# Dividing the probabilities by their sum before they are split and turned, in a top-k attention followed by two feed-forward layers

## The chip, the cores and the metric

The kernel runs on one core of a Trainium2 chip. The metric is the device time of one execution, in microseconds. It is written for a planner that puts every engine's instructions in an order of its own, from priorities and a model of costs, and sets the waits between engines; each engine then works through its own queue strictly in that order. The engines are TensorE (PE, with PEld for the loading of weights), VectorE (DVE), ScalarE (ACT), GpSimd (POOL) and SyncE (SP), which issues the DMAs.

## The reference

Three steps follow each other. Attention over 4 batches x 8 heads x 576 positions x 64, in which each row keeps its 32 largest scores; then two feed-forward layers on the 2304 rows of 512.

```
scores = (q @ k.T) / 8
kth    = 32nd largest of each row
attn   = exp(where(scores >= kth, scores, -1e9) - max)
attn   = attn / (sum(attn) + 1e-9)
x      = heads of (attn @ v) side by side          # 2304 x 512
x      = (sigmoid(x @ w_gate) * (x @ w_val)) @ w_out   # inner size 1536
out    = relu(x @ w_in)**2 @ w_out2                    # inner size 2048
```

## The kernel before

The 2304 rows are 18 row blocks of 128. Six chunks of one block come first, then six chunks of two blocks (`CHUNKS`). A chunk goes through attention and then through the two layers. Attention works in units: one row block and one head, eight per block, 144 in all. Heads go in pairs (j = 0 and 1), because two heads of 64 fill 128 partitions.

A unit has these steps. `head` loads what is needed and calls `scores` (L349): f32 matmuls, and ScalarE copies the 128x576 scores into a score tile `S` (L371). `softmax` (L374) lets VectorE look for the 32 largest: four times MAX8 (L383), three times MATCH_REPLACE8 (L390). `marks` keeps these four MAX8. Then GpSimd makes the threshold (L398) and the offset (L399), ScalarE masks (L402, Prelu) and takes the exponential.

From chunk 6 on (`TCI`), that is in the last 96 units, the probabilities are not divided there. GpSimd adds 10 ln 2 to the offset (L406), ScalarE takes the exponential twice, once as f16 into the unit's own score tile (L412) and once as f32 with its sum (L413). GpSimd subtracts one from the other, in two pieces (L417, L420), so that the score tile holds a high and a low f16 part. A DMA that turns the tile writes it into `PT` (L436). After the second head of a pair GpSimd scales both sums by a factor of the values (L427).

`tail` for two units earlier calls `values16` (L494): VectorE takes one over the two sums (L499), TensorE multiplies the turned probabilities with the values (L508), and then spreads the two inverse sums over 64 partitions each with f32 matmuls against the identity (L520). ScalarE copies product and spread (L529), GpSimd multiplies them (L531), and the result is split in two f16 parts (L533, L534).

In the early chunks (0 to 5) the probabilities are divided at once: exponential with sum, GpSimd, reciprocal on VectorE (L444), product on GpSimd (L453).

The layers (`moe`, L787) work on 256 inner columns at a time: `l1_pair` makes the gate and value products (L766) and a tile of activations in two f16 parts (L781, L782), `l1_acc` multiplies it into the chunk's second input (L806). `l2_pair` and `l2_acc` do the same for layer two (L869, L878 to L882, L890). The tiles of activations have the tag `hi`, with `HIB` of them; output tiles `ob` (L907) use the same tag. Between the layers the input is measured and split (L837 to L848), and `nxt`, from chunk `PRE0` on, starts the first two column pairs of the next chunk in that place.

The order of the work is set by emission and priority. The units of attention are emitted ahead of the layers: `LEAD` units ahead of the chunk that is in the layers, `LEAD2` from chunk `PRE0` on. Within a unit, `late` emits the next unit's `head`, pending splits of values, and the `tail` of two units ago, all of it with higher priority than the unit's own threshold and exponential. Two marks hold things back in the order: the reciprocal not before the second MAX8 of the unit that is searched (`marks[1]`), the value matmuls not before its last (`marks[3]`).

Score tiles have the tag `S`, with `SB` of them; the staging of keys and values (`prep_keys` L145, `prep_values` L186) uses the same tag.

Of the kernel before, what the change touches and what calls it, by code (L numbers as in the profile page):

```python
# [2 lines left out]

# [6 lines left out]
F16 = mybir.dt.float16  # L10
BF16 = mybir.dt.bfloat16
F32 = mybir.dt.float32
# [3 lines left out]
AF = mybir.ActivationFunctionType  # L16
ALU = mybir.AluOpType
# [5 lines left out]
P = 128  # L23
# [1 line left out]
NEG = -3.0e38  # L25
BIG = float(2.0**100)
M4 = 3
HIB = 3
DEPTH2 = 2
CHUNKS = [[0], [1], [2], [3], [4], [5]] + [[i, i + 1] for i in range(6, 18, 2)]  # L30
AHEAD = 1000
LEAD = 9
CA0 = -5.0
CA = 6.0
CW = 3.0
# [3 lines left out]
PLAIN = (0,)  # L39
KST = 3  # L40
NPRE = 2
PRE0 = 6
X2W = 3
LEAD2 = 14
TD = 7
# [17 lines left out]
LOP = 3  # L63
LOA = 0
TCI = 6
SB = 4
XRB = 1
PB = 10

# [5 lines left out]
def tile_topk_attention__then__two_moe_layers(  # L75
# [14 lines left out]
    nc = tc.nc  # L90
    B, H, S, D = q.shape
# [6 lines left out]
    NHP = H // 2  # L98
# [19 lines left out]

    ident = const.tile([P, P], F32, name="ident")
    make_identity(nc, ident)  # L120
    ones = const.tile([P, P], BF16, name="ones")
    nc.vector.memset(ones, 1.0)


    def pow2_scale(norm, name, pool=mpool, tag=None, bufs=None, squared=True, s=None):
# [130 lines left out]
    def xfac(ci, b):  # L256


        if ci not in xfacs:
            bs_ = batches(ci)  # L260
            vf = vsc.bitcast(F32)
            ix = mpool.tile([P, 1], F32, tag="xsc", bufs=3, name=f"ix_{ci}")
            nc.vector.reduce_max(ix, vf[:, bs_[0] * NHP : (bs_[-1] + 1) * NHP, 1], axis=AX.X)

            nc.gpsimd.tensor_scalar(ix, ix, 2.0, None, op0=ALU.mult)
            fs = {}
            for b_ in bs_:
                f = mpool.tile([P, NHP], F32, tag="xfc", bufs=4, name=f"xfc_{ci}_{b_}")
                nc.gpsimd.tensor_scalar(
                    f, vf[:, b_ * NHP : (b_ + 1) * NHP, 0], ix, 1.0, op0=ALU.mult, op1=ALU.mult  # L270
                )
                fs[b_] = f
            xfacs[ci] = ix, fs
        return xfacs[ci][1][b]

    class Pair:


        def __init__(self, ci, hp, xt):
            self.ci, self.hp, self.xt = ci, hp, xt  # L280
            self.tts = chunks[ci]
            self.N = len(self.tts) * P
            self.segs = segments(ci)
            self.vt, self.kt, self.qt, self.pt, self.ends, self.sums = {}, {}, {}, {}, {}, {}

        def load(self):
            ci, hp = self.ci, self.hp
# [86 lines left out]
        def softmax(self, j, i, ss, late=None):  # L374
# [26 lines left out]
            )  # L401
            nc.scalar.activation(wk, ss, AF.Prelu, bias=bs[:, 0:1], scale=1.0, alpha=BIG)  # L402
            if self.ci >= TCI:


                nc.gpsimd.tensor_scalar(  # L406
                    bs[:, 1:2], bs[:, 1:2], float(PB * math.log(2.0)), None, op0=ALU.add
                )
                if j == 0:
                    self.sums[i] = apool.tile([P, 2], F32, tag="rz", bufs=3, name=f"z_{tt}_{self.hp}")  # L410
                pp = ss.bitcast(F16)
                nc.scalar.activation(pp[:, 0:S], wk, AF.Exp, bias=bs[:, 1:2], scale=SCALE)  # L412
                nc.scalar.activation(  # L413
                    wk, wk, AF.Exp, bias=bs[:, 1:2], scale=SCALE,
                    accum_out=self.sums[i][:, j : j + 1],
                )
                nc.gpsimd.tensor_tensor(  # L417
                    pp[:, S + ST : 2 * S], wk[:, 0:SM], pp[:, 0:SM], op=ALU.subtract
                )
                nc.gpsimd.tensor_tensor(  # L420
                    pp[:, S : S + ST], wk[:, SM:S], pp[:, SM:S], op=ALU.subtract
                )
                if j == 1:

                    z = self.sums[i]
                    for b, _, o, n in pieces(tt):
                        nc.gpsimd.tensor_scalar(  # L427
                            z[o : o + n],
                            z[o : o + n],
                            float(1e-9 * 2.0**PB),  # L430
                            xfac(self.ci, b)[o : o + n, self.hp : self.hp + 1],
                            op0=ALU.add,
                            op1=ALU.mult,
                        )
                pt = apool.tile([P, 2 * CB + 1, P], F16, tag="PT", bufs=3, name=f"PT_{tt}_{h}")
                nc.sync.dma_start_transpose(pt, pp)  # L436
                self.pt[(j, i)] = pt
                return None
# [13 lines left out]
            for o, x in ((self.ends[i][:, j], wk[:, SM:S]), (wk[:, 0:SM], wk[:, 0:SM])):  # L452
                nc.gpsimd.tensor_scalar(o, x, rz, 1.0, op0=ALU.mult, op1=ALU.mult)  # L453
            return wk, ident

        def transpose(self, j, i, wk, dg):
            tt = self.tts[i]
# [33 lines left out]
                )  # L491
                nc.scalar.copy(self.pe[:, i * P : (i + 1) * P], tq[:, 0:P])

        def values16(self, i, after=None, summed=None):  # L494
            tt = self.tts[i]
            xp = ps_t.tile([P, 512], F32, tag="tr", name=f"xp_{tt}_{self.hp}")

            z = self.sums[i]
            rc = nc.vector.reciprocal(z, z)  # L499
            if summed is not None:  # L500
                tc.add_manual_dep(rc.ins, summed.name, NOSYNC, reason="summed by then")

            terms = [(a, c, c) for c in range(CB + 1) for a in range(2)]
            terms += [(0, c, CB + 1 + c) for c in range(CB)]
            for b, _, o, n in pieces(tt):
                for x, (a, c, pc) in enumerate(terms):
                    for j in range(2):
                        mm = nc.tensor.matmul(  # L508
                            xp[j * D : (j + 1) * D, o : o + n],
                            self.vt[b][:, j, a, c],  # L510
                            self.pt[(j, i)][:, pc, o : o + n],
                            start=(o == 0 and x == 0),
                            stop=(x == len(terms) - 1),
                            skip_group_check=True,
                        )
                        if after is not None:
                            tc.add_manual_dep(mm.ins, after.name, NOSYNC, reason="lands by then")
                            after = None
            for j in range(2):
                nc.tensor.matmul(  # L520
                    xp[j * D : (j + 1) * D, P : 2 * P],
                    z[:, j : j + 1].to_broadcast([P, D]),
                    ident,
                    start=False,
                    stop=True,
                    skip_group_check=True,
                )
# [182 lines left out]
    def split_act(src, name, xs, N):  # L710

        sq = xs[:, 1].bitcast(BF16)
        nc.scalar.activation(sq, src, AF.Square)
        pq = ps_t.tile([P, 512], F32, tag="tr", name=name + "pq")
        for c in range(KM):
            nc.tensor.matmul(pq[:, 0:N], ones, sq[:, c], start=(c == 0), stop=(c == KM - 1))
        cm = mpool.tile([P, 1], F32, tag="xcm", bufs=2, name=name + "cm")
# [69 lines left out]
    def moe(ci, nxt=None):  # L787
# [45 lines left out]
        with tc.high_priority(offset=XUP):  # L833
            sq = x2[:, 1].bitcast(BF16)
            pq = ps_w.tile([P, 512], F32, tag="wk", name=f"x2pq_{ci}")
            for h in range(2):
                nc.scalar.activation(sq[:, h * KH : (h + 1) * KH], srcs[h], AF.Square)  # L837
                for c in range(h * KH, (h + 1) * KH):
                    nc.tensor.matmul(pq[:, 0:N], ones, sq[:, c], start=(c == 0), stop=(c == KM - 1))
            cm = mpool.tile([P, 1], F32, tag="cm", bufs=2, name=f"x2cm_{ci}")  # L840
# [181 lines left out]
    def attention():  # L1022
# [55 lines left out]
                nxt = pairs[pi + 1]  # L1078
                nxt.queries(nxt.tts[0:1])

        def tail(n, after=None, summed=None):
            pr, pi, j, i = units[n]
            if pr.ci >= TCI and j == 0:
                return
# [21 lines left out]
                        )  # L1106
            pr.xt = xts[pr.ci]
            if pr.ci >= TCI:
                pr.values16(i, after, summed)
# [14 lines left out]
        for n, (pr, pi, j, i) in enumerate(units):  # L1124
# [18 lines left out]
            work[n] = pr.softmax(j, i, ready.pop(n), late)  # L1143
            yield
        for n in range(len(units) - 2, len(units)):
            tail(n)
        yield
# [51 lines left out]
    for ci in PLAIN:  # L1199
        n = 0  # L1200
# [92 lines left out]
```

## Time and profile before

| | |
|---|---|
| median of 3 runs | 1302.67 us (1301.55 to 1307.42) |
| profiled execution, its own time | 1302.77 us |
| its span | 1301.0 us |
| PE busy | 1185.3 us (91%) |
| DVE busy | 978.3 us (75%) |
| POOL busy | 852.3 us (66%) |
| ACT busy | 816.7 us (63%) |
| granted TensorE clock, mean | 0.95 |

The span is the time from the first to the last instruction that the profiler saw. Busy time of an engine is the union of its instructions. A wait in the lists is idle time of an engine ahead of an instruction, put down to the event that came last. Lines as L520 are lines of the kernel before. A f32 matmul is recorded as two. Shares of busy time are means over stages; the stages differ here, as the rows show.

### The profile page before, as it was taken

To read this page: it belongs to the slowest core of one execution; us is meant where nothing else is said; L and a number is where in the kernel's file an instruction comes from. 1 tells how busy PE (TensorE), PEld (TensorE's weight loads), DVE (VectorE), ACT (ScalarE), POOL (GpSimd) and SP (SyncE) were. 2 spreads that over 40 slices of the span, in tenths; PEclk is the share of its full clock that TensorE was granted. 3 is DMA by queue.
4 is the path that set the end of the run, shared out by engine and by line. 5 is a ranking of instruction groups with operands and counts; after the bars stand their busy time and mean duration, and the time that the engine had idled before them with its cause. 6 is when DMAs were issued, how large, how long until landed. Compare 5 with 4: busy or idle time off the path is not lost.

```text
span 1301.0 us, 31666 instructions
## 1 busy us (share of the span) xinstructions
PE 1185.3 (91%) x11901; PEld 955.4 (73%) x11901; DVE 978.3 (75%) x1954; ACT 816.7 (63%) x1714; POOL 852.3 (66%) x1450
## 2 busy tenths in 40 slices
PE   6756989878999898998988999999999999999998
PEld 5545877666888778786877778867876887787775
DVE  6999989999759978799879779999999976010010
ACT  4877777777667676767666766767677656222122
POOL 1888879877657486767666867787678657315223
PEclk9557999988999999998999999999999999999999
DMA  7979762222454355555566556446544523100000
GB/s 185 348 264 307 248 180 63 73 64 76 135 143 114 96 138 138 128 136 115 146 132 135 118 142 136 115 113 175 95 98 102 117 44 51 26 2 1 17 1 17
DMA packets 243194, 154.00 MB, mean 118 GB/s; under 512 B 193120, under 2 KB 209504, under 8 KB 243040
## 3 DMA queue, kind: packets, MB, share of 16 engines
q1 hardware_dynamic: 243040, 151.97, 44.7%
q8 instruction: 94, 1.54, 0.5%
q14 instruction: 60, 0.49, 0.1%
HBM read 105.51 MB, written 18.09 MB: 95 GB/s over the span
## 4 chain that ended last, share of the span: by engine, by line
PE 55%; DVE 12%; POOL 11%; DMA 8%; ACT 6%; issue 5%; SPq 2%; POOLq 0%; ACTq 0%; DVEq 0%
PE ph L869 11%; PE acc L890 10%; PE pv L766 7%; PE pg L766 7%; PE acc L806 7%; PE sp L368 5%; DVE mx L383 4%; DVE W L390 3%; DMA PT<-S 3%; POOL S L417 2%; PE xp L508 2%; PE xp L546 2%; DMA wg_r<-in_moe_w_gate_dram 2%; POOL rh L882 1%; ACT W L413 1%
## 5 line engine op out<-in xcount | busy, mean ns | idle before, releaser
L383 DVE MAX8 mx<-W 128x8 f32<-128x576 f32 x432 | 327.5, 758 | 10.6
L869 PE MATMUL ph<-x,wi_w 128*128 128x256 f16 (+1 forms) x2112 | 210.6, 254 | 9.5 <-ACT x L845 8.3
L390 DVE MATCH_REPLACE8 W<-mx,W 128x576 f32<-128x576 f32 x288 | 213.8, 742 | 0.0
L869 PEld LDWEIGHTS <-wi_w 128*128 128x128 f16 x2112 | 172.9, 100 | 40.7 <-issue 11.6
L890 PE MATMUL acc<-w_w,rh 128*128 128x512 f16 x816 | 195.5, 379 | 1.9 <-POOL rh L882 1.9
L402 ACT ACTIVATE W<-S,bs 128x576 f32<-128x576 f32 x144 | 111.6, 775 | 105.2 <-POOL bs L398 104.6
L417 POOL TENSOR_TENSOR S<-W,S 128x512 f16<-128x512 f32 x96 | 111.3, 1159 | 80.2 <-ACT W L413 79.2
L766 PE MATMUL pg<-xs,wg_w 128*128 128x256 f16 (+1 forms) x1584 | 156.4, 249 | 1.1 <-POOL xs L534 1.1
L766 PE MATMUL pv<-xs,wv_w 128*128 128x256 f16 (+1 forms) x1584 | 154.7, 249 | 0.6 <-ACT th L776 0.4
L368 PE MATMUL sp<-kst,qt 128*128 128x288 f32 x608 | 136.8, 339 | 16.1 <-ACT S L371 4.6
L778 DVE TENSOR_TENSOR th<-pv,th 128x512 f32<-128x512 f32 (+1 forms) x66 | 37.1, 562 | 137.6 <-PE pv L766 126.5
L766 PEld LDWEIGHTS <-wg_w 128*128 128x128 f16 x1584 | 126.5, 98 | 18.5 <-issue 2.4
L806 PEld LDWEIGHTS <-wo_w 128*128 128x128 f16 x1584 | 127.5, 99 | 14.2 <-issue 2.0
L766 PEld LDWEIGHTS <-wv_w 128*128 128x128 f16 x1584 | 125.3, 98 | 15.3 <-issue 2.4
L890 PEld LDWEIGHTS <-rh 128*128 128x128 f16 x816 | 77.0, 98 | 77.4 <-POOL rh L882 2.2
L371 ACT COPY S<-sp 128x576 f32<-128x576 f32 x144 | 91.4, 635 | 61.2 <-PE sp L368 33.5
L806 PE MATMUL acc<-gh,wo_w 128*128 128x128 f16 (+1 forms) x1344 | 126.1, 247 | 0.8 <-POOL gh L782 0.6
L383 DVE MAX8 mx<-S 128x8 f32<-128x576 f32 x144 | 107.2, 744 | 24.2 <-ACT S L371 22.7
L368 PEld LDWEIGHTS sp<-kst,qt 128*128 128x128 f32 x608 | 94.8, 201 | 28.8 <-ACT S L371 8.1
L881 POOL TENSOR_TENSOR r<-r 128x512 f32<-128x512 f32 (+1 forms) x88 | 74.3, 845 | 62.7 <-ACT rh L880 61.7
L390 DVE MATCH_REPLACE8 W<-mx,S 128x576 f32<-128x576 f32 x144 | 106.9, 742 | 0.0
L882 POOL TENSOR_TENSOR rh<-r,rh 128x512 f16<-128x512 f32 (+1 forms) x88 | 83.3, 948 | 4.2
(304 smaller groups left out, 2240.5 us busy)
## 6 DMA issues: line engine op xcount, KB each, us to landing
kst<-ks SPq DMA_DIRECT2D x112, 288.0 KB, 3.1
v<-vd SPq DMA_DIRECT2D x32, 320.0 KB, 3.3
qn<-in_q_dram SPq DMA_DIRECT2D x128, 64.0 KB, 2.3
wi_r<-in_moe_w_in_dram SPq DMA_DIRECT2D x16, 512.0 KB, 5.2
w_r<-in_moe_w_out_dram SPq DMA_DIRECT2D x16, 512.0 KB, 4.6
v<-in_v_dram SPq DMA_DIRECT2D x56, 128.0 KB, 2.3
wg_r<-in_moe_w_gate_dram SPq DMA_DIRECT2D x12, 512.0 KB, 8.5
wv_r<-in_moe_w_val_dram SPq DMA_DIRECT2D x12, 512.0 KB, 6.9
```

The source lines that it names most:

```text
L368: nc.tensor.matmul(sp[:, e, 0:HALF], l, r, start=(x == 0), stop=(x == len(ops) - 1))
L371: nc.scalar.copy(ss.rearrange("p (e s) -> p e s", e=2), sp[:, :, 0:HALF])
L383: m8 = nc.vector.max(mx[:, r], cur)
L390: nc.vector.match_replace(wk, mx[:, r], cur, NEG)
L402: nc.scalar.activation(wk, ss, AF.Prelu, bias=bs[:, 0:1], scale=1.0, alpha=BIG)
L417: nc.gpsimd.tensor_tensor(pp[:, S + ST : 2 * S], wk[:, 0:SM], pp[:, 0:SM], op=ALU.subtract)
L766: nc.tensor.matmul(pp[:, e * N : (e + 1) * N], wblk(wd, a, c, f0, P), xs[:, b_, c, :], start=(e == 0 and n == 0), stop=(n == 3 * KM - 1), ...
L806: nc.tensor.matmul(acc[:, d // 2, (d % 2) * N : (d % 2 + 1) * N], wblk("wo", a, f, d * P, P), gh[:, b_, e * N : (e + 1) * N], start=(f == ...
L869: nc.tensor.matmul(ph[:, e * N : (e + 1) * N], wblk("wi", a, c, f0, P), x2[:, b_, c, :], start=(e == 0 and n == 0), stop=(n == 3 * KM - 1) ...
L881: nc.gpsimd.tensor_tensor(r, r, r, op=ALU.mult)
L882: nc.gpsimd.tensor_tensor(gh[:, 1], r, gh[:, 0], op=ALU.subtract)
L890: nc.tensor.matmul(acc2[:, i, 0:DM], gh[:, b_, e * N + i * P : e * N + (i + 1) * P], wblk("w2", a, f, 0, DM), start=(f == 0 and x == 0), s ...
```

## The change

In the last 96 units the f32 exponential with its sum is taken first and alone. GpSimd scales the unit's own sum at once. A new step, `turn16`, comes one unit later: a reciprocal on VectorE, not before the third MAX8 of the next unit (`marks[2]`); a copy to f16 on ScalarE with the inverse as its scale; the same product in f32 on GpSimd, in place; the two subtractions and the turning DMA as before. The value matmuls then give the final result up to a power of two, so that the spread of the inverse sums over the partitions (L520) and its product (L531) are gone, and two ScalarE copies with a constant scale take their place.

With it come other sizes: five score tiles instead of four, two tiles of activations instead of three, a column of ones that is broadcast instead of a 128x128 tile, one buffer instead of two for two small maxima, a result tile of half the size, `LEAD` 10 instead of 9, and `PRE0` 4 instead of 6.

```
-HIB = 3
+HIB = 2
-LEAD = 9
+LEAD = 10
-PRE0 = 6
+PRE0 = 4
-SB = 4
+SB = 5
...
-    ones = const.tile([P, P], BF16, name="ones")
-    nc.vector.memset(ones, 1.0)
+    one = const.tile([P, 1], BF16, name="ones")
+    nc.vector.memset(one, 1.0)
+    ones = one.to_broadcast([P, P])
...
             if self.ci >= TCI:
-                nc.gpsimd.tensor_scalar(
-                    bs[:, 1:2], bs[:, 1:2], float(PB * math.log(2.0)), None, op0=ALU.add
-                )
...
-                nc.scalar.activation(pp[:, 0:S], wk, AF.Exp, bias=bs[:, 1:2], scale=SCALE)
...
+                nc.scalar.activation(
+                    wk, wk, AF.Exp, bias=bs[:, 1:2], scale=SCALE, accum_out=bs[:, 2:3]
+                )
+                for b, _, o, n in pieces(tt):
+                    nc.gpsimd.tensor_scalar(
+                        bs[o : o + n, 3:4], bs[o : o + n, 2:3], 1e-9,
+                        xfac(self.ci, b)[o : o + n, self.hp : self.hp + 1],
+                        op0=ALU.add, op1=ALU.mult,
+                    )
+                return ss, wk, bs
...
+        def turn16(self, j, i, ss, wk, bs, summed):
+            tt = self.tts[i]
+            h = 2 * self.hp + j
+            rz = apool.tile([P, 1], F32, tag="rz", bufs=3, name=f"rz_{tt}_{h}")
+            rc = nc.vector.reciprocal(rz, bs[:, 3:4])
+            if summed is not None:
+                tc.add_manual_dep(rc.ins, summed.name, NOSYNC, reason="summed by then")
+            pp = ss.bitcast(F16)
+            nc.scalar.activation(pp[:, 0:S], wk, AF.Copy, scale=rz)
+            nc.gpsimd.tensor_scalar(wk, wk, rz, 1.0, op0=ALU.mult, op1=ALU.mult)
+            for o, f, e in ((S + ST, 0, SM), (S, SM, S)):
+                nc.gpsimd.tensor_tensor(pp[:, o : o + e - f], wk[:, f:e], pp[:, f:e], op=ALU.subtract)
+            pt = apool.tile([P, 2 * CB + 1, P], F16, tag="PT", bufs=3, name=f"PT_{tt}_{h}")
+            nc.sync.dma_start_transpose(pt, pp)
+            self.pt[(j, i)] = pt
...
-            z = self.sums[i]
-            rc = nc.vector.reciprocal(z, z)
...
-            for j in range(2):
-                nc.tensor.matmul(
-                    xp[j * D : (j + 1) * D, P : 2 * P],
-                    z[:, j : j + 1].to_broadcast([P, D]),
-                    ident,
...
-            xr = apool.tile([P, 2 * P], F32, tag="xr", bufs=XRB, name=f"xr_{tt}_{self.hp}")
-            nc.scalar.copy(xr, xp[:, 0 : 2 * P])
-            xf = xr[:, 0:P]
-            nc.gpsimd.tensor_tensor(xf, xf, xr[:, P : 2 * P], op=ALU.mult)
+            xf = apool.tile([P, P], F32, tag="xr", bufs=XRB, name=f"xf_{tt}_{self.hp}")
             hi, lo = (self.xt[:, a, self.hp, i * P : (i + 1) * P] for a in range(2))
-            nc.scalar.copy(hi, xf)
+            for t in (hi, xf):
+                nc.scalar.activation(t, xp[:, 0:P], AF.Copy, scale=float(2.0**-PB))
             nc.gpsimd.tensor_tensor(lo, xf, hi, op=ALU.subtract)
...
                 def late(marks, n=n, pr=pr):
+                    if units[n - 1][0].ci >= TCI:
+                        turn(n - 1, marks[2])
                     if pr.ci >= TCI:
                         head(n + 1)
...
-                        tail(n - 2, marks[3], marks[1])
+                        tail(n - 2, marks[3])
```

## Rows read from the trace of the kernel before

**Rows 1.** Windows, all engines: stretch, length, busy us (count) of each, clock, DMA, GB/s.
```profile
0.00:325.00 325.00, 253.91 (x2084) 206.40 (x2085) 301.31 (x540) 237.00 (x462) 245.88 (x293) 0.84 0.57 181
325.00:488.00 163.00, 155.62 (x2049) 133.18 (x2047) 127.09 (x299) 111.56 (x282) 106.92 (x232) 0.98 0.47 125
488.00:1106.00 618.00, 589.01 (x6306) 473.54 (x6304) 537.10 (x1089) 423.76 (x900) 439.47 (x866) 0.99 0.52 118
1106.00:1301.00 195.00, 186.82 (x1472) 142.24 (x1470) 12.78 (x27) 44.39 (x73) 60.05 (x62) 0.99 0.04 11
```

**Rows 2.** Waits, 488 to 1106 us: who waited for whom, us, times, longest.
```profile
POOL S L417 <- ACT W L413: 79.2, 50, 4.5
ACT W L402 <- POOL bs L398: 75.1, 54, 3.0
...
ACT S L371 <- DMA PT<-S: 17.3, 19, 2.4
...
PE sp L368 <- ACT S L371: 4.6, 10, 0.7
...
PE kpt L164 <- DMA kn<-in_k_dram: 4.4, 3, 2.3
...
PE sp L368 <- DMA kst<-ks: 4.0, 2, 2.3
...
PE ph L869 <- ACT x L845: 3.5, 1, 3.5
```

**Rows 3.** Timeline of PE around one pair of heads: start us, us, instruction.
```profile
646.45 0.39 PE L520 MATMUL xp<-ident,z 128*64 128x128 f32 x4
646.76 0.79 PE L368 MATMUL sp<-kst,qt 128*128 128x288 f32 x4
```

**Rows 4.** Instructions on the sums `z`: count, ns min/median/max.
```profile
L520 PE MATMUL xp<-ident,z x192: 272/275/422, 484.6 to 1113.1; 128*64 128x128 f32 x192
L427 POOL TENSOR_SCALAR z<-z,xfc x52: 258/265/268, 477.5 to 1107.5; 128x2 f32<-128x2 f32 x44, 64x2 f32<-64x2 f32 x8
```

**Rows 5.** Groups by line and form, 488 to 1106 us: busy us, mean ns, idle before.
```profile
L417 POOL TENSOR_TENSOR S<-W,S 128x512 f16<-128x512 f32 x92 | 106.6, 1159 | 80.2 <-ACT W L413 79.2
...
L413 ACT ACTIVATE W<-W,bs 128x576 f32<-128x576 f32 x92 | 71.6, 778 | 1.2
...
L420 POOL TENSOR_TENSOR S<-W,S 128x64 f16<-128x64 f32 x91 | 27.8, 306 | 0.0
...
L531 POOL TENSOR_TENSOR xr<-xr 128x128 f32<-128x128 f32 x46 | 21.0, 456 | 10.8 <-ACT xr L529 9.5
...
L406 POOL TENSOR_SCALAR bs<-bs 128x1 f32<-128x1 f32 x92 | 19.9, 217 | 7.7
```

**Rows 6.** Line L453, the product of the early chunks.
```profile
L453 POOL TENSOR_SCALAR W<-W,rz x32: 684/692/697, 227.0 to 456.7; 128x512 f32<-128x512 f32 x32
```

**Rows 7.** Line L444, the reciprocal of the early chunks, and its engine's wait (us, times).
```profile
L444 DVE RECIPROCAL rz<-bs x48: 138/154/166, 22.0 to 455.4; 128x1 f32<-128x1 f32 x48
...
  POOL bs L443: 10.1, 10
```

**Rows 8.** Timeline of all engines, one unit's end and the next unit's search.
```profile
638.83 0.76 DVE L383 MAX8 mx<-W 128x8 f32<-128x576 f32 x1
...
643.06 0.78 ACT L402 ACTIVATE W<-S,bs 128x576 f32<-128x576 f32 x1 [2.56 <-POOL bs L398]
...
643.49 0.75 DVE L383 MAX8 mx<-W 128x8 f32<-128x576 f32 x1
...
646.33 0.19 ACT L413 ACTIVATION_READ_ACCUMULATOR W<-W,bs 128x1 f32 x1
```

**Rows 9.** Line L383, MAX8 on the working copy, whole span.
```profile
L383 DVE MAX8 mx<-W x432: 737/761/764, 13.6 to 1099.6; 128x8 f32<-128x576 f32 x144
```

**Rows 10.** DMA issues: count, median us from issue to landing.
```profile
PT<-S SPq DMA_TRANSPOSE x96, 2.9
```

**Rows 11.** Chain that ended last, one piece in the last stage: start, us.
```profile
1186.67 2.62 PE ph L869 x24
```

More of the change, by code (lines that the diff above doesn't have):

```diff
@@ L1 @@
-import math
 from contextlib import ExitStack
@@ L269, in xfac @@
                 nc.gpsimd.tensor_scalar(
-                    f, vf[:, b_ * NHP : (b_ + 1) * NHP, 0], ix, 1.0, op0=ALU.mult, op1=ALU.mult
+                    f,
+                    vf[:, b_ * NHP : (b_ + 1) * NHP, 0],
+                    ix,
+                    float(2.0**-PB),
+                    op0=ALU.mult,
+                    op1=ALU.mult,
                 )
@@ L283, in __init__ @@
             self.segs = segments(ci)
-            self.vt, self.kt, self.qt, self.pt, self.ends, self.sums = {}, {}, {}, {}, {}, {}
+            self.vt, self.kt, self.qt, self.pt, self.ends = {}, {}, {}, {}, {}
         def load(self):
@@ L403, in softmax @@
             if self.ci >= TCI:
-                nc.gpsimd.tensor_scalar(
-                    bs[:, 1:2], bs[:, 1:2], float(PB * math.log(2.0)), None, op0=ALU.add
-                )
-                if j == 0:
-                    self.sums[i] = apool.tile([P, 2], F32, tag="rz", bufs=3, name=f"z_{tt}_{self.hp}")
-                pp = ss.bitcast(F16)
-                nc.scalar.activation(pp[:, 0:S], wk, AF.Exp, bias=bs[:, 1:2], scale=SCALE)
-                nc.scalar.activation(
-                    wk, wk, AF.Exp, bias=bs[:, 1:2], scale=SCALE,
-                    accum_out=self.sums[i][:, j : j + 1],
-                )
[L417 to L423, printed above, removed]
-                    z = self.sums[i]
[L426 to L438, printed above, removed]
+                nc.scalar.activation(
+                    wk, wk, AF.Exp, bias=bs[:, 1:2], scale=SCALE, accum_out=bs[:, 2:3]
+                )
+                for b, _, o, n in pieces(tt):
+                    nc.gpsimd.tensor_scalar(
+                        bs[o : o + n, 3:4],
+                        bs[o : o + n, 2:3],
+                        1e-9,
+                        xfac(self.ci, b)[o : o + n, self.hp : self.hp + 1],
+                        op0=ALU.add,
+                        op1=ALU.mult,
+                    )
+                return ss, wk, bs
             nc.scalar.activation(
@@ L492, in transpose, with values16 @@
                 nc.scalar.copy(self.pe[:, i * P : (i + 1) * P], tq[:, 0:P])
-        def values16(self, i, after=None, summed=None):
+        def values16(self, i, after=None):
             tt = self.tts[i]
             xp = ps_t.tile([P, 512], F32, tag="tr", name=f"xp_{tt}_{self.hp}")
-            z = self.sums[i]
-            rc = nc.vector.reciprocal(z, z)
-            if summed is not None:
-                tc.add_manual_dep(rc.ins, summed.name, NOSYNC, reason="summed by then")
             terms = [(a, c, c) for c in range(CB + 1) for a in range(2)]
@@ L716, in split_act @@
             nc.tensor.matmul(pq[:, 0:N], ones, sq[:, c], start=(c == 0), stop=(c == KM - 1))
-        cm = mpool.tile([P, 1], F32, tag="xcm", bufs=2, name=name + "cm")
+        cm = mpool.tile([P, 1], F32, tag="xcm", bufs=1, name=name + "cm")
         nc.vector.reduce_max(cm, pq[:, 0:N], axis=AX.X)
@@ L839, in moe @@
                     nc.tensor.matmul(pq[:, 0:N], ones, sq[:, c], start=(c == 0), stop=(c == KM - 1))
-            cm = mpool.tile([P, 1], F32, tag="cm", bufs=2, name=f"x2cm_{ci}")
+            cm = mpool.tile([P, 1], F32, tag="cm", bufs=1, name=f"x2cm_{ci}")
             nc.vector.reduce_max(cm, pq[:, 0:N], axis=AX.X)
@@ L1079, in head, with turn, tail @@
                 nxt.queries(nxt.tts[0:1])
-        def tail(n, after=None, summed=None):
+        def turn(n, summed=None):
+            pr, pi, j, i = units[n]
+            pr.turn16(j, i, *work.pop(n), summed)
+        def tail(n, after=None):
             pr, pi, j, i = units[n]
@@ L1108, in tail @@
             if pr.ci >= TCI:
-                pr.values16(i, after, summed)
+                pr.values16(i, after)
             else:
@@ L1140, in late @@
                     if units[n - 2][0].ci >= TCI:
-                        tail(n - 2, marks[3], marks[1])
+                        tail(n - 2, marks[3])
             work[n] = pr.softmax(j, i, ready.pop(n), late)
             yield
+        turn(len(units) - 1)
         for n in range(len(units) - 2, len(units)):
```

4 lines of the change are left out of this document (removed).

## The prediction

> **What bounds the kernel now.** I read the stages first: busy time of each engine in four stretches [rows 1]. The reader is to see that two engines share the role. Up to 325 us VectorE is busy 301.3 of 325 us and TensorE waits for it (253.9 us busy, granted clock 0.84). From 325 us on TensorE is the bound: 155.6 of 163 us, then 589.0 of 618 us while the twelve later row blocks go through attention, then 186.8 of 195 us with nothing but the two layers. VectorE in the long third stage is at 537.1 of 618 us, so it has 80.9 us to spare there and TensorE only 29.0 us. After 325 us, then, time is TensorE's work plus its waits: taking a matmul away there pays in full as long as no new wait fills the hole, and a busier ScalarE (423.8 us) or GpSimd (439.5 us) costs only what reaches TensorE as a wait.
>
> Next the list of waits in the third stage [rows 2]. The reader is to see two kinds. The long ones are between ScalarE and GpSimd: GpSimd stands 79.2 us ahead of the split of the probabilities (L417) until the second exponential is summed, ScalarE 75.1 us ahead of L402 until GpSimd has made the threshold. They are two sides of one loop through two in-order queues, and they do not reach TensorE as such. The short ones do: score matmuls behind the copy of scores that waits for a score tile (4.6 us), the turning of keys behind its load (4.4 us), score matmuls behind the keys' load (4.0 us), and the start of layer two behind L845 (3.5 us).
>
> The third view is the timeline of TensorE at one pair of heads, and the count of the matmuls that go [rows 3, 4].
>
> **The change part by part.**
>
> *The spread of one over the sums.* Per row block and pair of heads two f32 matmuls go (L520), four records. In the queue they hold the next matmul from 646.45 to 646.76 us, 0.31 us. The trace has 192 records, 48 such groups: 48 x 0.31 = 14.9 us less for TensorE, all of it in the stage where it is the bound. I take it whole: -14.9 us.
>
> *The same division on other engines.* Per unit (row block and head, 96 of them) ScalarE keeps its count: one exponential with sum instead of two, and a scaled copy to f16 of the same 128x576 in place of the one that went; L413 shows 778 ns for that size [rows 5]. After the value matmuls there are two 128-column copies where there were one of 256 columns and one of 128: no gain that I count. GpSimd loses the add L406 (0.217 us) per unit and the product L531 (0.456 us) per pair [rows 5], and gains the product of 128x576 by one over the sum. The nearest row is the same operation on 128x512 in the early chunks, 692 ns [rows 6]; by columns 0.78 us. It also scales the sum per unit instead of per pair: 52 more instructions at 0.265 us [rows 4]. Together 96 x (0.78 - 0.217) + 52 x 0.265 - 48 x 0.456 = 54.0 + 13.8 - 21.9 = +45.9 us on GpSimd, which has 178.5 us to spare in the stage. Its cover is that spare time: nothing, if it stays off TensorE's path; the loop below is what it costs if the cover is gone.
>
> VectorE does 96 reciprocals instead of 48: 48 x 0.15 = 7 us [rows 7], inside its 80.9 us.
>
> Weighed against a rule: MAX8 and MATCH_REPLACE fill VectorE, and L383 takes 737 to 764 ns over 432 of them while GpSimd is busy seven tenths of the time [rows 9]. So no search here was held for the length of a GpSimd product. The Trainium skill, "SBUF — State Buffer", section "SBUF: two separate sides", says that GpSimd and VectorE take a shared pair of ports in turn, each for a whole instruction, and that it concerns VectorE operations with two SBUF inputs or in a two-port mode. If the searches came under it, the new products could hold VectorE for up to 96 x 0.78 = 75 us; by the row they hold it for none, and the sum goes by the row.
>
> *The added wait.* The reciprocal of a unit now stands in VectorE's queue behind the third maximum of the next unit, and behind it stand that unit's last replacement and maximum. Look at one unit [rows 8]: its last maximum ends at 639.6 us, its sum is there at 646.5 us, and the next unit's third maximum ends at 644.2 us. Without the second exponential (0.78 us) and the wait between the two, the sum would be there at about 643.06 + 0.78 + 0.97 = 644.8, scaled by 645.1 us: 0.9 us later than the earliest place of the reciprocal. So the bounds are 0 (put after the last replacement or maximum) and 96 x 0.9 = 86 us of VectorE. The nearest row is the reciprocal L444 of the early chunks, the same chain of exponential, GpSimd and reciprocal: 10.1 us of waiting in 48 [rows 7], 0.21 us each. For 96 that is 20 us. TensorE shows 29.0 us idle where VectorE shows 80.9, 0.36 of it, so I charge 0.36 x 20 = +7 us (bounds 0 and 0.36 x 86 = 31).
>
> ScalarE's scaled copy waits for the reciprocal, and behind it in ScalarE's queue stands the copy of the next scores, for which the next search waits; what that costs is part of the same +7. GpSimd's product in place, the two subtractions and the turning DMA come after. SP's queue holds its DMA issues in order too, so loads issued behind a turning DMA shift with it; the chain is longer by 0.15 + 0.78 + 0.78 - 0.78, about 0.9 us, against the value matmuls that come two units later: no cost counted.
>
> *Five score tiles.* A score tile is held until its turning DMA has landed, 2.9 us after issue [rows 10]. The added links hold it about 1 to 2 us longer; the fifth tile gives a whole unit more, 618/92 = 6.7 us. The key and value staging uses the same tiles. TensorE's waits that hang on them are the 4.6, 4.4 and 4.0 us above, 13.0 us. Bounds: 0 (these loads are late for other reasons) to 13.0; I take half, -6.5 us.
>
> *Two tiles of activations.* A pair of layer two takes 2.62 us of matmuls for the first product [rows 11] and about as much for the second, in turn. With two tiles the square of pair n must wait until the second product of pair n-2 has ended, one such stretch after its own matmuls; its result is wanted four stretches, 10.5 us, after them. Square, product and difference in that time are cheap (below 3.5 us: three operations of at most L417's 1.16 us). Cost 0, up to 0.5 us at each of 11 chunk ends (5.5 us) if the cover is gone, because the output tiles share them.
>
> *Earlier start of the next chunk (chunks 4 and 5 too), one unit more of lead.* The first two column pairs of the next chunk fill the gap before layer two. The gap it can fill is that of 3.5 us [rows 2], one single stall ahead of layer two; bounds 0 to 3.5, I take -2. Loss: the order of units against layers moves, but TensorE is the bound there and the work is the same. In the first stage more tiles and more lead may shift work; VectorE has 23.7 us idle there, I take 0 and keep a third of that, 8 us, on either side. The broadcast column of ones and the single small buffers: 0.
>
> Sum: the profiled execution took 1302.8 us (span 1301.0 plus 1.8), which is within 0.2 us of the median 1302.67. 1302.8 - 14.9 - 6.5 - 2 + 7 = 1286.4. **1286 us.** Its own range, with the terms of the tiles, the stall and the wait going either way, is 1278 to 1294.
>
> **Rivals.**
>
> *Everything frees up.* All 13.0 us and all 3.5 us go and the reciprocal costs nothing: 1302.8 - 14.9 - 13.0 - 3.5 = 1271. For it: the waits on score tiles are many (19 of ScalarE for the turning DMA, 17.3 us). Against: keys also wait for loads and stores of their own.
>
> *The hole is filled.* TensorE does 14.9 us less and waits that much more, since VectorE's pace holds it: 537.1 + 7 + 20 = 564 of then 603 us still leaves 39 us, which speaks against; that the searches stand in strict order speaks for. The score tiles' -6.5 goes against the wait's +7, and only the -2 is left: 1301.
>
> *The loop becomes the pace (slower).* One loop through the queues: reciprocal 0.15, copy 0.78, product 0.78, subtractions 1.16 and 0.31, threshold 0.22, Prelu 0.78, exponential with sum 0.97, scaled sum 0.27, and the reciprocal again: 5.4 us [rows 4 to 8], the threshold taken as L406, and with an estimated 0.07 us between neighbours (10 of them) 6.1 us. It closes only if a unit's threshold stands behind the previous unit's subtractions in GpSimd's queue. GpSimd's other work, (439.5 + 45.9)/92 - 2.74 = 2.5 us per unit, can lie in it: 6.1 to 8.6 us, against 6.7 - 0.16 = 6.56 us that TensorE then needs per unit. It decides from 6.56 us on. The loop of now, 4.2 us bare, is already closed in 50 of 92 units (the count of the 79.2 us). At the middle, 7.35 us, 50 units lose 0.8 us each, 40 us: 1302.8 - 14.9 - 6.5 + 40 = 1321. For it: the two long waits [rows 2]. Against: where the reciprocal is late the threshold can stand first, and the loop is open.
>
> **How the numbers follow.** Forecast 0.42, everything frees up 0.20, hole filled 0.16, loop 0.22. No change means within 0.5%, 6.5 us, about what a measurement of this kernel can tell: 1296 to 1309. Faster: the forecast nearly whole and the first rival, 0.62; same: the hole filled, less a little on either side, 0.15; slower: the loop and a worse front, 0.23. The range runs from just below the first rival, with some of the front's 8 us, to most of the loop's price: 1262 to 1318.
>
> **What would show it.** Right: no f32 matmul after the value matmuls; TensorE's busy time in attention of the later chunks down by about 15 us and its idle time not above 29; few waits of the score copy on the turning DMA; a GpSimd product near 0.78 us; VectorE waiting for the scaled sum some 20 us in all. The loop: VectorE waiting far more than that at the reciprocal, score copies late, TensorE idle ahead of score and value matmuls by tens of us, the last search ending after 1106 us. The forecast is wrong if TensorE's idle time rises by 15 us or more, or if the first 325 us move by more than 8.

## The result and the profile after

| | before | after |
|---|---|---|
| median of 4 runs | 1303.82 us (1301.55 to 1307.42) | 1290.03 us (1285.39 to 1293.53) |
| ratio | | 0.989, 95% interval 0.985 to 0.993 |
| profiled execution, span | 1301.0 us | 1287.5 us |

The forecast was 1286 us, faster. The profiled execution of after took 1289.27 us. Run again beside other kernels, after had the ratio 0.9866 (0.985 to 0.9883) to before.

First the stretches of after, as in [rows 1] (busy us and count of PE, PEld, DVE, ACT, POOL; clock; DMA; GB/s).

```profile
0.00:325.00 325.00, 251.85 (x2041) 204.17 (x2042) 299.55 (x540) 235.61 (x458) 241.45 (x290) 0.84 0.57 181
325.00:488.00 163.00, 155.60 (x2053) 131.37 (x2051) 127.77 (x301) 110.30 (x279) 106.53 (x229) 1.00 0.45 118
488.00:1106.00 618.00, 594.57 (x6222) 476.16 (x6220) 536.96 (x1135) 423.25 (x907) 485.65 (x878) 0.99 0.54 119
1106.00:1287.50 181.50, 173.49 (x1402) 133.64 (x1399) 12.77 (x27) 42.83 (x71) 56.10 (x59) 0.99 0.04 13
```

The reader is to see where the 13.5 us of span went. They do not show in the pace of attention: VectorE is busy 537.0 us in the third stretch as before, and the last search ends at 1101.0 us (1100.4 before). TensorE does more in the same 618 us, 594.6 us against 589.0, although it has less to do per unit: it gets further ahead with the layers, and what is left of them after attention is 181.5 us instead of 195.0. So the freed time is cashed in at the end.

Fewer matmuls are not the whole of it. After 325 us TensorE is idle 38.8 us in after and 44.5 us before (length less busy time, over three rows), 5.7 us less. And its granted clock is higher: after 325 us the clock records show the lower of the two levels for 14.3 us instead of 27.3, with TensorE busy in 12.4 and 25.2 us of them. The same layer matmul (128x256) starts every 109 ns at the upper level and every 213 ns at the lower, so an estimated 6.4 us came back there, half of the difference. A second profiled execution of after has 37.8 us idle and 11.4 us busy at the lower level.

The waits of after in the third stretch, as in [rows 2]: first of all engines, then of TensorE alone.

```profile
ACT S L450 <- DVE rz L446: 41.7, 45, 2.3
POOL W L451 <- ACT S L450: 38.6, 32, 2.9
ACT W L407 <- POOL bs L403: 35.8, 43, 2.6
...
ACT S L376 <- DMA PT<-S: 14.9, 14, 2.0
```
```profile
PE xp L505 <- DMA PT<-S: 7.7, 3, 3.8
PE sp L373 <- DMA kst<-ks: 3.5, 3, 1.6
PE kpt L164 <- DMA kn<-in_k_dram: 3.2, 4, 1.3
PE acc L876 <- POOL rh L868: 2.7, 2, 2.1
...
PE ph L855 <- ACT x L831: 0.6, 1, 0.6
PE sp L373 <- ACT S L376: 0.2, 1, 0.2
```

L505 is the line of the value matmuls, L446 the new reciprocal, L450 the scaled copy, L451 the product, L376 the copy of scores. The old loop between GpSimd and ScalarE (79.2 and 75.1 us) has become a chain over three engines with shorter waits. On TensorE the waits for score tiles and keys went from 13.0 to 6.9 us, and a new one stands at the top: value matmuls waiting for turned probabilities (5.6 us in the second profiled execution of after).

The new chain of one unit, and the wait at its end, in the timeline (all engines, 681.4 to 690 us), with the stretch behind the wait:

```profile
681.46 0.16 DVE L446 RECIPROCAL rz<-bs 128x1 f32<-128x1 f32 x1 [0.18 <-POOL bs L414]
...
681.71 0.78 ACT L450 ACTIVATE S<-W,rz 128x576 f16<-128x576 f32 x1 [1.00 <-DVE rz L446]
...
682.67 0.74 POOL L451 TENSOR_SCALAR W<-W,rz 128x576 f32<-128x576 f32 x1
...
683.59 1.42 POOL L453 TENSOR_TENSOR S<-W,S 128x512 f16<-128x512 f32 x2
...
685.04 1.31 SPq L455 DMA_TRANSPOSE PT<-S  x1
...
685.25 0.24 PE L505 MATMUL xp<-PT,v 128*64 128x128 f16 x1
...
689.26 1.02 PE L505 MATMUL xp<-PT,v 128*64 128x128 f16 x19 [3.77 <-DMA PT<-S]
```
```profile
689.50:696.30 6.80, 5.63 (x46) 4.00 (x41) 6.60 (x14) 4.60 (x11) 4.99 (x10) 0.50 0.55 131
```

From the reciprocal to the landing that releases TensorE are 7.8 us. The first value matmul has the first head's tile; the second head's is still on its way. The wait costs twice: right behind it the granted clock is at its lower level (0.50) for 6.8 us. Over the 96 units (each one's end of search against the landing of its turning DMA, both from the timeline) the median from search to landing is 14.0 us, against 10.3 us before.

### The profile page after: what moved, and what is told of

The parts are those of the page before. It is cut to its first block, busy times and chain, and to the rows that moved or that the text cites. A ratio compares the mean times of both kernels' runs of the same rounds, so it can differ in the third digit from the quotient of the medians.

```text
span 1287.5 us, 31379 instructions
## 1 busy us (share of the span) xinstructions
PE 1175.5 (91%) x11709; PEld 945.3 (73%) x11709; DVE 977.1 (76%) x2002; ACT 812.0 (63%) x1714; POOL 889.7 (69%) x1454
## 3 DMA queue, kind: packets, MB, share of 16 engines
q1 hardware_dynamic: 243040, 151.97, 45.9%
## 4 chain that ended last, share of the span: by engine, by line
PE 50%; DVE 20%; POOL 8%; DMA 8%; issue 6%; ACT 5%; SPq 2%; POOLq 0%; ACTq 0%; DVEq 0%
PE ph L855 11%; PE acc L876 10%; DVE mx L388 8%; DVE W L395 7%; PE pv L752 6%; PE pg L752 6%; PE acc L792 6%; PE sp L373 4%; PE xp L505 3%; DMA PT<-S 2%; PE xp L532 2%; DMA ve<-in_v_dram 1%; DMA vd<-vom 1%; POOL S L453 1%; POOL rh L868 1%
## 5 line engine op out<-in xcount | busy, mean ns | idle before, releaser
L855 PE MATMUL ph<-x,wi_w 128*128 128x256 f16 (+1 forms) x2112 | 206.6, 251 | 5.1 <-ACT x L831 4.5
L876 PE MATMUL acc<-w_w,rh 128*128 128x512 f16 x816 | 198.5, 380 | 5.5 <-POOL rh L868 5.5
L373 PE MATMUL sp<-kst,qt 128*128 128x288 f32 x608 | 136.2, 335 | 12.9 <-DMA kst<-ks 4.5
L453 POOL TENSOR_TENSOR S<-W,S 128x512 f16<-128x512 f32 x192 | 136.7, 734 | 2.1
L376 ACT COPY S<-sp 128x576 f32<-128x576 f32 x144 | 91.7, 637 | 55.8 <-PE sp L373 38.0
L867 POOL TENSOR_TENSOR r<-r 128x512 f32<-128x512 f32 (+1 forms) x88 | 74.3, 845 | 63.4 <-ACT rh L866 57.5
L792 PE MATMUL acc<-gh,wo_w 128*128 128x128 f16 (+1 forms) x1248 | 114.3, 244 | 1.1 <-POOL gh L768 0.8
L450 ACT ACTIVATE S<-W,rz 128x576 f16<-128x576 f32 x96 | 74.4, 775 | 48.7 <-DVE rz L446 44.9
```

Source lines behind the costliest of these rows:

```text
L373: nc.tensor.matmul(sp[:, e, 0:HALF], l, r, start=(x == 0), stop=(x == len(ops) - 1))
L376: nc.scalar.copy(ss.rearrange("p (e s) -> p e s", e=2), sp[:, :, 0:HALF])
L450: nc.scalar.activation(pp[:, 0:S], wk, AF.Copy, scale=rz)
L453: nc.gpsimd.tensor_tensor(pp[:, o : o + e - f], wk[:, f:e], pp[:, f:e], op=ALU.subtract)
L792: nc.tensor.matmul(acc[:, d // 2, (d % 2) * N : (d % 2 + 1) * N], wblk("wo", a, f, d * P, P), gh[:, b_, e * N : (e + 1) * N], start=(f == ...
L855: nc.tensor.matmul(ph[:, e * N : (e + 1) * N], wblk("wi", a, c, f0, P), x2[:, b_, c, :], start=(e == 0 and n == 0), stop=(n == 3 * KM - 1) ...
```

## The experiments

Each was timed beside before on the same chip, and ratios are to before. The runs took three chips. After itself ran again on one of them, beside experiments 7 and 9 and the second half of 4; its 0.9866 is used throughout, so elsewhere a difference to it goes across chips. With the 0.989 of the first measurement such differences are some 3 us smaller.

**1. The sizes alone.** Before, with all sizes of after.

```
-HIB = 3  LEAD = 9   PRE0 = 6  SB = 4
+HIB = 2  LEAD = 10  PRE0 = 4  SB = 5     (and the column of ones, single small buffers)
```

> The kernel before with all sizes of the kernel after (five score tiles, two tiles of activations, LEAD 10, PRE0 4, column of ones, single small buffers), the division as before. Theory A (the gain is TensorE's matmuls of the spread; sizes only trim waits): 1296 to 1303 us against 1303.8 of before. Theory B (the sizes make the gain, the moved division gives nothing): 1288 to 1293 us.

0.9943 (0.9921 to 0.9966), 1297.6 us. This is theory A's range, but the sizes are clearly worth something: 0.57% of 1304 us, 7.4 us.

**2. The division with the old sizes.** The column of ones and the single small buffers stay as in after.

```
-HIB = 2  LEAD = 10  PRE0 = 4  SB = 5
+HIB = 3  LEAD = 9   PRE0 = 6  SB = 4     (in the kernel after)
```

> The kernel after with the old sizes of four (score tiles 4, activations 3, LEAD 9, PRE0 6). Theory A: 16 us of matmuls are gone but score tiles are held some 4 us longer with one tile less: 1292 to 1299 us. Theory B: 1302 to 1308 us.

1.021 (1.0188 to 1.0232), 1332.5 us: slower than before by more than either theory allowed. The moved division needs something among the sizes.

**3. Which size it needs.** After with four score tiles, all else as it is.

```
-SB = 5
+SB = 4
```

> The kernel after with four score tiles instead of five, all else as after. If the longer hold of a score tile (the turned tile lands 14.0 us after the search in the middle of 96 units, 10.3 us before) is what made the division with the old sizes slow: ratio to before 1.008 to 1.022. If the old order or the third tile of activations did that: 0.987 to 0.995.

1.0233 (1.0216 to 1.0251), just above the range of the first theory. It is the fifth tile. The stretch of attention and the waits of four_tiles:

```profile
488.00:1106.00 618.00, 560.05 (x5780) 450.64 (x5780) 496.12 (x1052) 390.99 (x845) 442.33 (x811) 0.95 0.53 116
```
```profile
ACT S L376 <- DMA PT<-S: 57.5, 35, 4.0
```
```profile
PE sp L373 <- ACT S L376: 17.7, 9, 4.9
PE kpt L164 <- DMA kn<-in_k_dram: 14.6, 6, 4.8
PE xp L505 <- DMA PT<-S: 10.5, 6, 4.0
```

One of these waits of the score matmuls, and the stretch behind it:

```profile
597.54 0.79 PE L373 MATMUL sp<-kst,qt 128*128 128x288 f32 x4 [3.68 <-ACT S L376]
```
```profile
598.30:618.80 20.50, 10.48 (x87) 7.78 (x87) 17.34 (x35) 10.64 (x24) 12.81 (x26) 0.50 0.43 98
```

The copy of scores waits 57.5 us for tiles that the turning DMA still reads, and TensorE is busy only 560.1 us. A count fits it: from the copy into a score tile to the landing of its turning DMA are 22.2 us in the median before and 25.8 us after; with a unit every 6.7 us, that is 3.3 and 3.9 tiles held, and the staging of keys and values wants tiles of the same kind. Four were enough for the old chain and are not for the new one. The clock adds to the loss: right behind the wait shown it falls to 0.50 for 20.5 us, and it is 0.95 in the whole stretch. TensorE is idle 58.0 us of the 618 (23.4 in after) and busy 43.0 us at the lower level (9.1 in after), by the spacing of the matmuls above an estimated 17 us lost (half of the difference).

**4. The order alone, both ways.** After with the old lead and start, and before with the new ones.

```
 in after:   -LEAD = 10  PRE0 = 4   +LEAD = 9   PRE0 = 6
 in before:  -LEAD = 9   PRE0 = 6   +LEAD = 10  PRE0 = 4
```

> The kernel after with LEAD 9 and PRE0 6 as before; score tiles and activations as after. Theory A: 1289 to 1294 us, the earlier start of chunks 5 and 6 being worth 0 to 4 us. Theory B, with the order as the source: 1298 us or more.

> The kernel before with LEAD 10 and PRE0 4 alone, four score tiles, three tiles of activations. If the order pays by itself (chunks 5 and 6 are started in the gap ahead of layer two of chunks 4 and 5): ratio to before 0.992 to 0.997. If it pays only together with the fifth score tile: 0.998 to 1.004.

Taken from after: 0.995 (0.9931 to 0.997) against 0.9866, so the order is worth 0.84% there, 11 us (8 us against the 0.989); by its ratio, 1297 us, the run lies between the two ranges. Given to before: 1.0014 (1.0001 to 1.0027), nothing. The order pays only together with something else of the change. Whether that is a size or the division was not separated. The second and third stretch with the old order in after:

```profile
325.00:488.00 163.00, 154.20 (x1986) 130.86 (x1984) 125.53 (x291) 106.58 (x272) 104.13 (x224) 0.97 0.42 113
488.00:1106.00 618.00, 590.87 (x6164) 475.69 (x6163) 534.20 (x1134) 419.18 (x901) 478.69 (x867) 0.98 0.54 119
```

The last search ends at 1111.6 us instead of 1101.0. After 325 us TensorE is idle 43.9 us (38.8 in after) and busy 31.1 us at the lower clock (12.4). So the order buys fewer waits and a higher clock; why it does not in before (43.9 us and 22.0 us, against 44.5 and 25.2) is open.

**5. The spread alone.** Before without its f32 spread matmuls; the results are left undivided.

```
-            for j in range(2):
-                nc.tensor.matmul(xp[j * D : (j + 1) * D, P : 2 * P],
-                                 z[:, j : j + 1].to_broadcast([P, D]), ident, ...)
...
-            nc.scalar.copy(xr, xp[:, 0 : 2 * P])
+            nc.scalar.activation(
+                xr.rearrange("p (a n) -> p a n", a=2),
+                xp[:, 0:P].unsqueeze(1).to_broadcast([P, 2, P]),
...
```

> The kernel before without its f32 spread matmuls (L520); the results are left undivided, the copy and the product behind them stay with the same sizes. Theory A (TensorE's queue gives its 16 us back wherever they go): ratio to before 0.986 to 0.990. Theory C, formed after the spread was put back into the kernel after at no cost (the hole fills with waits for the turned tiles or for the searches): ratio 0.994 to 1.003.

0.9923 (0.9905 to 0.9941): 0.77%, 10.0 us, between the two ranges. The timeline of TensorE tells why not 15. First before, then without the spread:

```profile
645.64 0.97 PE L508 MATMUL xp<-PT,v 128*64 128x128 f16 x28
```
```profile
647.61 0.97 PE L508 MATMUL xp<-PT,v 128*64 128x128 f16 x28
648.51 0.54 PE L368 MATMUL sp<-kst,qt 128*128 128x288 f32 x2
```

With the spread, the score matmuls follow at 646.76 us [rows 3], 1.12 us after the first value matmul; without it 0.90 us after. The same two figures are the medians over the groups of 28 that no wait breaks, 31 in each run. The difference is 0.22 us, not the 0.31 us that the spread itself holds the queue: the spread starts 0.81 us after the first value matmul, what follows without it only at 0.90 us, so 0.09 us of the step to other matmuls stays. 48 x 0.22 = 10.6 us, and 10.0 us is what came.

**6. The spread put back into after.**

```
+            for j in range(2):
+                nc.tensor.matmul(xp[j * D : (j + 1) * D, P : 2 * P],
+                                 ident[:, j : j + 1].to_broadcast([P, D]), ident, ...)
```

> The kernel after with two f32 matmuls per row block and pair put back behind the value matmuls (a column of the identity spread into unused columns; their result is not used). Theory A (TensorE's queue is the bound, each group costs what it holds): 1290 + 15 = 1305 us. Rival (VectorE paces the stage, since the last search ends at 1101 us in both kernels, so matmuls there are free): 1288 to 1294 us.

0.9893 (0.9871 to 0.9914), 1291.9 us. Against after's 0.9866 that is some 3.5 us more, and the intervals overlap: theory A's 1305 us is far off. The waits of TensorE show what filled the place:

```profile
PE xp L505 <- DMA PT<-S: 0.8, 1, 0.8
```

In after the value matmuls wait 7.7 us for turned tiles, with the spread put back 0.8 us. The planned order is another one too, so this is not shown to be the whole difference.

A comparison with experiment 1, on the same chip, says more: there before has all the sizes of after and its own spread, at 0.9943 (0.9921 to 0.9966). This kernel has the same sizes and as many f32 matmuls and is 0.5% faster, 6.5 us, with intervals that do not overlap. That part of the gain came with the moved division and not from fewer matmuls on TensorE. Its trace shows TensorE idle 34.1 us after 325 us (37.5 with the sizes alone) and busy 9.9 us at the lower clock (21.6). Why the moved division leaves fewer such falls was not tested.

To see whether matmuls are free there at all:

**7. Twice the spread in after** (`for j in (0, 1, 0, 1)`).

> The kernel after with four f32 matmuls per row block and pair put in (twice as many as were taken out, 32 us of TensorE's queue; their result is not used). If TensorE's queue has no slack beyond the waits for turned tiles that the first two filled (some 14 us): ratio to before 1.000 to 1.004. If matmuls at this place are free: 0.987 to 0.992.

1.0064 (1.004 to 1.0089), 25.8 us above after, somewhat above the range of the first theory. An unbroken group takes 0.90 us without the f32 matmuls, 1.12 us with two and 1.34 us with four, so each lot adds 0.22 us to a group, 10.6 us in all. The first lot cost some 3.5 us, the second 22 us. So they are not free; the first lot fell in part where TensorE would have waited. The second costs about twice its own length: the last search ends at 1124.4 us (1098.9 with one lot), and after 325 us TensorE is idle 42.5 us (34.1) and busy 19.5 us at the lower clock (9.9).

**8. A second product on GpSimd in after.**

```
             nc.gpsimd.tensor_scalar(wk, wk, rz, 1.0, op0=ALU.mult, op1=ALU.mult)
+            nc.gpsimd.tensor_scalar(wk, wk, 1.0, 1.0, op0=ALU.mult, op1=ALU.mult)
```

> The kernel after with a second GpSimd product of 128x576 by 1.0 in every later unit, 96 x 0.75 = 72 us more for GpSimd and 0.75 us more in the chain to the turned tile. Cover theory (GpSimd's time is hidden): ratio to before 0.988 to 0.993. Loop theory (the chain of reciprocal, copy, product and subtractions is near the pace of a unit): 1.005 to 1.03.

1.0057 (1.0035 to 1.0078): 24.9 us above after, for 96 products of 0.67 us, 64 us. The time is neither hidden nor passed on in full.

```profile
ACT S L376 <- DMA PT<-S: 32.9, 23, 5.3
```
```profile
PE xp L506 <- DMA PT<-S: 11.5, 6, 5.1
```

Landing comes 16.2 us after the search (14.0 in after), a score tile is held 28.7 us, and the mean period of a unit, from one end of a search to the next, grows from 6.74 to 7.08 us. So a little more on this chain slows attention. Whether the one product of after does so already is not shown by this.

**9. The product on ScalarE in after.**

```
-            nc.gpsimd.tensor_scalar(wk, wk, rz, 1.0, op0=ALU.mult, op1=ALU.mult)
+            nc.scalar.activation(wk, wk, AF.Copy, scale=rz)
```

> The kernel after with the f32 product by one over the sum on ScalarE (0.78 us, a second scaled copy) instead of GpSimd, which gives GpSimd 72 us back and leaves the chain as long. If GpSimd's queue (threshold and subtractions behind each other) is what holds the chain: ratio to before 0.977 to 0.986. If the chain's own length is: 0.988 to 0.996, ScalarE being delayed as much as GpSimd is freed.

0.9907 (0.9891 to 0.9923), the second theory's range: no better than after, and slightly worse.

```profile
PE 1175.9 (91%) x11709; PEld 945.6 (73%) x11709; DVE 973.9 (75%) x2002; ACT 874.0 (68%) x1810; POOL 821.4 (64%) x1358
```

GpSimd has 68 us less than in after and ScalarE 62 us more. The landing is 1.1 us earlier (12.9 us), and ScalarE's copies of scores pay for it: TensorE's wait for them is 6.3 us instead of 0.2.

**10. Value matmuls later in after.**

```
-                    if units[n - 2][0].ci >= TCI:
-                        tail(n - 2, marks[3])
+                    if units[n - 3][0].ci >= TCI:
+                        tail(n - 3, marks[2])
```

> The kernel after with the value matmuls placed behind the third maximum of the unit after (three units behind the search instead of two, tail(n - 3, marks[2])), nothing else changed. Theory C (TensorE waits some 14 us for turned tiles at the value matmuls, and that ate most of the 16 us): ratio to before 0.975 to 0.984. Rival (those waits are chance of one execution, or come back at the layers' start): 0.987 to 0.993.

0.9976 (0.9963 to 0.999): both theories missed, it is worse than after by 1.1%. The waits at the value matmuls are gone, but two others came:

```profile
PE pg L752 <- ACT xs L519: 8.7, 2, 5.0
PE kpt L164 <- DMA kn<-in_k_dram: 7.6, 3, 4.2
PE sp L373 <- ACT S L376: 5.2, 9, 1.9
```

Layers start later behind the later results, and the copy of scores waits 29.3 us for turning DMAs instead of 14.9, score tiles being held 28.1 us. That the turned tiles (three of them) are freed later is a likely cause of the longer hold; it was not tested.

No version beat after.

## Why the prediction was right, point by point

**The number and the sum.** 1286 us was forecast, 1290 us came, and the direction was right. The terms did not come as they were summed: some were too large, one gain had no term, and they offset each other, so the closeness is partly luck. Of the signs named, TensorE's idle time in the third stretch stayed below 29 us (23.4), but its busy time there rose by 5.6 us instead of falling by 15; over the whole span it fell by 9.8 us (1185.3 to 1175.5).

**TensorE's time counts.** Half right. The search keeps its pace, and the time is gained in the layers. The count of 14.9 us took the spread's own hold of the queue; with the step to the next matmuls it is 10.6 us, and alone it paid 10.0 us. This term was a third too large. In after the matmuls are worth still less: put back, they cost some 3.5 us. The condition that the prediction named, that no new wait fills the hole, did not hold: the value matmuls wait for turned tiles. The 6.5 us that came with the moved division at the same count of matmuls, and the higher clock after 325 us, stand in no term of the sum.

**Five score tiles.** As a trim of waits the term was right: the three waits lost 6.1 us (13.0 to 6.9), forecast 6.5. What the prediction did not see is that the tile is a condition: without it the change is 3.7% slower (1.0233 against 0.9866). By the count of tiles held that follows from the next step.

**"The chain is longer by about 0.9 us: no cost counted."** This step failed. The landing comes 3.7 us later (10.3 to 14.0 us). I had added durations and left out the queues. In medians over the 96 units, counted from the end of the search: before, the sum is there at 5.0 us and the turning DMA is issued at 7.0 us. In after the sum is there at 3.6 us, but it is scaled only by 4.7 us, the reciprocal starts at 5.3 us (the next unit's third maximum ends at 4.0 us), the product ends at 8.0 us, and the issue comes at 10.3 us. That is 3.3 us later, where the added durations, with the scaled sum that was not in them, make 1.2 us; the rest are waits in the engines' queues. The last 0.4 us do not come from the division: issue to landing takes 3.3 us instead of 2.9 [rows 10], and it does so with the old division and the new sizes too, but not with the new order alone. First sizes_only, then order_only:

```profile
DMA to landing us min/median/max: 3.2/3.4/5.9
```
```profile
DMA to landing us min/median/max: 2.8/2.9/5.8
```

The longer chain shows as 7.7 us of waits at the value matmuls, and by the count in experiment 3 it is what makes the fifth tile necessary.

**The wait of the reciprocal.** Forecast 20 us on VectorE and 7 us on TensorE; measured:

```profile
L446 DVE RECIPROCAL rz<-bs x96: 142/145/165, 470.4 to 1106.6; 128x1 f32<-128x1 f32 x96
...
  POOL bs L414: 7.6, 9
```

7.6 us in 9 waits. VectorE is hardly held; ScalarE is, 41.7 us behind the reciprocal, though TensorE's wait for the copies of scores fell all the same (4.6 to 0.2 us). Some 7 us of waits came on TensorE, but at the value matmuls, so two errors of mine offset each other. That is luck.

**The product.** Sized right:

```profile
L451 POOL TENSOR_SCALAR W<-W,rz x96: 732/745/757, 472.6 to 1107.7; 128x576 f32<-128x576 f32 x96
```

0.745 us (0.78 forecast), GpSimd up by 37.4 us over the span (852.3 to 889.7; 45.9 forecast). That it costs nothing was not tested by itself: a second one costs 24.9 us (experiment 8), and moving the one to ScalarE gains nothing (experiment 9).

**The rule on the shared ports and the searches.** After, with the products beside them, MAX8 is as before [rows 9]:

```profile
L388 DVE MAX8 mx<-W x432: 734/761/764, 13.9 to 1100.2; 128x8 f32<-128x576 f32 x144
```

The Trainium skill, "SBUF — State Buffer", section "SBUF: two separate sides", limits the shared ports to VectorE operations with two SBUF inputs or in a two-port mode; MAX8, with one input, bears that out here, with a median of 761 ns in both kernels.

**Two tiles of activations.** Forecast nothing; TensorE's wait for them in the third stretch went from 1.4 to 2.7 us. Over all the time after 325 us, its waits for the tiles of both layers went from 2.0 to 6.3 us. The 4.3 us more are within the 5.5 us allowed as an upper bound, but not nothing; the number of tiles was not tested by itself.

**The order.** Forecast -2; the wait ahead of layer two did fall (3.5 to 0.6 us), but the order is worth 8 to 11 us in after. Mis-sized: not only that stall goes, but other waits and time at the lower clock (experiment 4).

**The rivals.** "Everything frees up" did not come: the waits for score tiles and keys are still 6.9 us. The loop as pace did not come with one product, and came in part with two. "The hole is filled" came in part, as the wait for turned tiles. The sum by measured parts: the spread alone 10.0 us and the sizes alone 7.4 us make 17.4 us, and after, run beside the others, gained 1.34%, 17.5 us. That they add up so well is chance and no explanation: in after the spread is worth 3.5 us and not 10.0, the moved division brings 6.5 us without it, and without the fifth tile the change loses.

What stays open: why the order helps in after and not in before, why the moved division itself gains 6.5 us with the clock higher, which size lengthens the landing (it shows in every kernel with the column of ones and the single small buffers, and in none without), and how much of spread_back's small cost is the changed plan and how much the filled waits.

## What to carry to other kernels

Price a removed group of matmuls from the start of what stands before it to the start of what follows, with and without it: a part of the step between kinds of matmuls stays. Then put the group back into the finished kernel: its worth there can be another one, as new waits fill the hole. When a step moves along a chain over several in-order queues, ask how long it then holds its buffer, divide by the period, and compare with the number of buffers, leaving room for others that use them; here the count was 25.8/6.7 = 3.9 against four, and a fifth tile made the difference between 2% slower and 1% faster. Test a size by itself in both kernels: the order was worth nothing in the old one and 8 to 11 us in the new one. And read the granted clock with the waits: a wait of TensorE can cost more than its own length.

## What the runs showed of the hardware

Two f32 matmuls over 64 stationary columns held TensorE's queue 0.31 us, but lengthened a group of 28 value matmuls by only 0.22 us, and two more by another 0.22 us (0.90, 1.12, 1.34 us). The product by a column of scalars on GpSimd took 745 ns for 128x576 f32, and the product by a constant 671 ns in the same place. The turning DMA of 128x1152 f16 landed a median 2.9 us after its issue before (shortest 2.8, longest 5.1 us) and 3.3 us in after (3.2 and 7.2 us), with the same issue; sizes_only has 3.4 us and order_only 2.9. The granted clock of TensorE fell to its lower level behind some of its waits: for 6.8 us behind 3.77 us in after, for 20.5 us behind 3.68 us in four_tiles. At that level the same layer matmul started every 213 ns instead of 109.
